# Merging five angles into the sine tables' instructions and reordering tile transposes in a gated state-space and feed-forward kernel

## The chip, the cores and the metric

The kernel runs on one core of one Trainium2 chip. The time is the device time of one execution in microseconds (us). A profile of one execution also has a span, from the first to the last instruction of the program; for this kernel it is about 1.8 us shorter than the time. TensorE is called PE in the profile, VectorE DVE, ScalarE ACT; PEld is PE's weight load.

## The reference

```python
x = A_x                                            # [1, 2048, 640], bf16
g = sigmoid((x * gate_w).sum(-1))                  # one gate per token
# a: state-space branch, 640 complex states
dt = exp(log_dt);  Lam_bar = exp(dt * (Lambda_re + 1j*Lambda_im))
h_t = Lam_bar * h_{t-1} + (B_bar @ x_t)            # over 2048 tokens
a = 2 * Re(C @ h) + x * Dskip
# b: feed-forward branch, 640 -> 1728 -> 640
b = gelu(x @ w1 + b1) @ w2 + b2
out = g * a + (1 - g) * b
```

## The kernel before

Tokens are handled in four chunks of 512, each of four tiles of 128. The recurrence is done by rotating with cosines and sines of `dt*Lambda_im*t`, so the kernel builds two tables, TCOS and TSIN, at its start. It takes sines for the first 64 angles of each state, then doubles the range three times with angle-addition formulas. These need the sine and cosine of five "span" angles (1, 512, 256, 128 and 64 steps).

Meanwhile PE must get going. The first chunk of x arrives with tokens on partitions and must be turned; PE does that with matmuls against an identity (`turn`), and DVE or ACT copies the result from PSUM to `xT[0]` (`turned`). Each of the four tiles has five 128-column blocks. `turn_first` does blocks 0 and 1, `turn_rest` blocks 2, 3 and 4. In the text, turn 2 is `turn_first(2)`, and the rest-turn of tile 2 is `turn_rest(2)`. Between turns PE does the feed-forward's first layer in strips: `part(kd, a)` is six matmuls of 128 columns into the six accumulators.

The kernel's PSUM pool has eight banks. Six are the accumulators, `pA` is a shared one, and so every `bank()` asked for by a turn gets the one that is left: a turn there must wait until the copy out of the turn before it has ended. I call it the rotating bank.

```python
def turn(p, col, a, kd):                                   # the matmul is L233 in the profile
    nc.tensor.matmul(p[:, col:col + P], lhsT=xn[0][:, a, kd*P:(kd+1)*P], rhs=ident[:], ...)

def turn_first(a, other):
    t = bank()
    turn(t, 0, a, 0)
    turned(nc.vector, t, 0, a, 0, 1)                       # DVE copy, L240
    turn(other, a * P, a, 1)
    turned(nc.scalar, other, a * P, a, 1, 2)               # ACT copy, L242
# ... cut ...
banks = [bank() for _ in range(FA)]                        # FA = 6 accumulators

def turn_rest(a, t, *parts):
    for k in range(KA, KD):                                # 2, 3, 4
        turn(t, (k - KA) * P, a, k)
    for engine, k0, k1 in parts:
        turned(engine, t, (k0 - KA) * P, a, k0, k1)
# ... cut; then the order in which PE gets its work (part's matmuls are L267):
part(0, 0); turn_first(1, pA); part(1, 0)
part(0, 1); turn_first(2, pA); part(1, 1)
turn_first(3, pA); part(0, 2)
turn_rest(0, bank(), (nc.scalar, KA, KD))
part(1, 2)
nc.tensor.matmul(pA[:, 0:3*KS], lhsT=prmA[:], rhs=ident[:, 0:3*KS], ...)   # the column matmul
nc.vector.tensor_copy(out=colA[:], in_=pA[:, 0:3*KS])
nc.scalar.activation(out=dt16[:], in_=ldt_c, func=ACT.Exp)                 # the dt exponential
# ... cut ...
part(0, 3)
turn_rest(1, bank(), (nc.vector, KA, KD))
part(1, 3)
turn_rest(2, pA, (nc.scalar, KA, KD))
part(2, 0)
turn_rest(3, bank(), (nc.vector, KA, KA + 1), (nc.scalar, KA + 1, KD))
# tables: u = angle in turns, kk = whole turns, red = rest, ab = |red|
nc.vector.tensor_tensor(out=u, in0=tf, in1=over(thp_c, HC), op=ALU.mult)    # 5 x 64 columns
nc.vector.tensor_copy(out=kk[:], in_=u)                                     # to int32
nc.vector.tensor_tensor(out=red, in0=u, in1=kk[:], op=ALU.subtract)
part(2, 1); part(2, 2); part(2, 3)
# ... two sine ACTIVATEs of 320 columns, then the same chain of 4 DVE and 2 ACT
#     instructions once more for the 5 x 5 span angles ...
```

## Time and profile before

| | before |
|---|---|
| time, median of 3 runs | 215.63 us (215.24 to 215.75) |
| span of the profiled run | 214.0 us |
| busy share | PE 98%, DVE 88%, ACT 48% |
| chain that ended last | PE 98% |
| 512-column matmuls, start to start | 215.6 ns |
| 128-column matmuls, start to start | 107 ns up to 5.5 us, 55.6 ns after |

The page of the kernel before has these lines on PE: busy time, share of the span and instructions, and further down the share of each engine in the chain of waits.

```profile
PE 210.5 (98%) x1407; PEld 126.5 (59%) x1407; DVE 189.4 (88%) x389; ACT 103.3 (48%) x188; POOL 1.0 (0%) x13
...
PE 98%; DVE 0%; issue 0%
```

PE is what bounds the kernel. "Busy" has to be read with care: a matmul's recorded duration (379 ns for 512 columns) is longer than the distance to the next (215.6 ns): the records of matmuls overlap, and the profile only models their ends. A short stall therefore hides inside the busy time. To find it one compares the start of a matmul with the start of the one before it. The timeline of the kernel before, from 5.7 to 9.4 us (columns: start in us, duration in us, engine, line, operation, names, shapes, count, and in brackets idle time before):

```profile
5.91 0.50 PE L267 MATMUL bank<-xT,w1a 128*128 128x128 bf16 x6
...
6.06 0.29 DVE L240 CAST xT<-bank 128x128 bf16<-128x128 f32 x1 [0.85 <-PE bank L233]
...
6.40 0.27 PE L233 MATMUL bank<-ident,xn 128*128 128x128 bf16 x2
...
6.51 0.50 PE L267 MATMUL bank<-xT,w1a 128*128 128x128 bf16 x6
6.66 0.29 DVE L240 CAST xT<-bank 128x128 bf16<-128x128 f32 x1 [0.31 <-PE bank L233]
...
7.00 0.33 PE L233 MATMUL bank<-ident,xn 128*128 128x128 bf16 x3
...
7.37 0.49 ACT L242 ACTIVATE xT<-bank 128x384 bf16<-128x384 f32 x1 [0.38 <-PE bank L233]
...
7.91 0.33 PE L233 MATMUL bank<-ident,xn 128*128 128x128 bf16 x3
...
8.94 0.33 PE L233 MATMUL bank<-ident,xn 128*128 128x128 bf16 x3
```

Six part matmuls start at 5.91, and 6 times 55.6 ns later, at 6.25, turn 3 could start; it starts at 6.40. That is just after DVE's copy of turn 2 (6.06 plus 0.29 is 6.35) has ended. The next turn likewise: 6.51 plus six matmuls is 6.85, and it starts at 7.00, after the copy that began at 6.66. From single matmuls, the stalls are 0.155 us at 6.40, 0.152 at 7.00, 0.046 at 7.91 and 0.032 at 8.94: 0.39 us, each at a turn. No bracket shows them, as PE counts as busy.

The table stage of the kernel before, in the same view:

```profile
10.03 0.33 DVE L387 CAST bu<-gel 128x320 int32<-128x320 f32 x1
...
11.33 0.47 ACT L392 ACTIVATE hs<-gel 128x320 f32<-128x320 f32 x1
11.33 0.18 DVE L395 TENSOR_TENSOR two<-thp_c,spans 128x25 f32<-128x25 f32 x1
...
12.16 0.21 ACT L400 ACTIVATE sq<-redq 128x25 f32<-128x25 f32 x1
...
12.59 1.28 ACT L272 ACT_TABLE_LOAD   x1
12.60 0.49 DVE L424 TENSOR_TENSOR gel<-hs,cq 128x320 f32<-128x320 f32 x1
```

L386 to L394 are the main chain, of 320 columns. L395 is the first of the span angles' own four instructions on DVE, L400 the first of their two on ACT, with 25 columns each; the four take 0.82 us from 11.33 to 12.15. L424 is the first doubling.

### The profile page before, as it was taken

Reading aid. Unit: us, or ns where it says so; the run is one execution under the profiler, and the core shown is the slowest. Engines: PE = TensorE matmul, PEld = TensorE weight load, DVE = VectorE, ACT = ScalarE, POOL = GpSimd, SP = SyncE. Lnnn points to the kernel's source line nnn. Section 1 sums busy time; section 2 is a strip of 40 time slices with the busy share of each in tenths; the row PEclk is TensorE's granted clock in tenths of the full one; section 3 lists DMA queues with packets and bytes.
Section 4 is the critical chain, followed back from the end, with each engine's and each line's share of the span. In section 5 each row is a group of like instructions: output and inputs, shape, how many; then the busy total and the mean of one; then the engine's idle time right before and its main releaser. Section 6 shows DMA issues by size and latency. Waiting matters only on the chain.

```text
span 214.0 us, 3599 instructions
## 1 busy us (share of the span) xinstructions
PE 210.5 (98%) x1407; PEld 126.5 (59%) x1407; DVE 189.4 (88%) x389; ACT 103.3 (48%) x188; POOL 1.0 (0%) x13
## 2 busy tenths in 40 slices
PE   8999999999999999999999999999999999999994
PEld 5945444454475644775457777444457687676773
DVE  2599999999998999999999999999999999993153
ACT  3599956675759579203573210455683422305100
POOL 1000000000000000000000000000000000000000
PEclk9999999999999999999999999999999999999999
DMA  6879999999000000052000006100000000110011
GB/s 192 222 178 190 201 156 246 347 207 230 1 0 0 3 0 0 14 152 96 0 0 3 0 0 180 68 0 2 3 0 14 0 3 31 61 34 0 0 66 61
DMA packets 31571, 15.84 MB, mean 74 GB/s; under 512 B 22978, under 2 KB 31554, under 8 KB 31554
## 3 DMA queue, kind: packets, MB, share of 16 engines
q1 hardware_dynamic: 30850, 14.99, 29.7%
q10 hardware_dynamic: 704, 0.62, 0.9%
q8 instruction: 11, 0.18, 0.4%
q14 instruction: 6, 0.05, 0.1%
HBM read 7.48 MB, written 2.62 MB: 47 GB/s over the span
## 4 chain that ended last, share of the span: by engine, by line
PE 98%; DVE 0%; issue 0%
PE bank L267 27%; PE bank L614 27%; PE bank L673 20%; PE bank L555 20%; PE bank L230 1%; PE bank L630 1%; PE bank L293 1%; PE bank L233 1%; DVE ot L678 0%; PE bank L362 0%; PE bank L283 0%; PE bank L404 0%; PE bank L373 0%
## 5 line engine op out<-in xcount | busy, mean ns | idle before, releaser
L614 PE MATMUL bank<-w_sb,gel 128*128 128x384 bf16 (+1 forms) x416 | 57.9, 300 | 0.0
L614 PEld LDWEIGHTS <-gel 128*128 128x128 bf16 x416 | 40.2, 98 | 17.1 <-issue 0.8
L558 ACT ACTIVATE bu<-bank 128x512 bf16<-128x512 f32 x40 | 23.7, 606 | 37.6 <-PE bank L555 37.6
L272 ACT ACTIVATE gel<-bank,colB 128x512 bf16<-128x512 f32 x52 | 33.6, 695 | 10.5 <-PE bank L267 10.2
L673 PEld LDWEIGHTS <-hs 128*128 128x128 bf16 x330 | 31.7, 98 | 11.7
L509 DVE TENSOR_TENSOR_SCAN g<-r_c,carry,v 128x512 bf16<-128x512 f32 x30 | 37.2, 1270 | 0.0
L622 ACT ACTIVATE gb<-bank,gcol 128x384 f32<-128x384 f32 (+1 forms) x32 | 15.1, 526 | 32.8 <-PE bank L614 16.6
L267 PE MATMUL bank<-xT,w1a 128*128 128x512 bf16 (+1 forms) x174 | 28.5, 319 | 0.0
L673 PE MATMUL bank<-CT_im,hs 128*128 128x320 bf16 (+2 forms) x165 | 27.1, 295 | 0.0
L673 PE MATMUL bank<-CT_re,hs 128*128 128x320 bf16 (+2 forms) x165 | 27.1, 295 | 0.0
L678 DVE SCALAR_TENSOR_TENSOR ot<-bank,gcol,gb 128x320 bf16<-128x320 f32 (+2 forms) x33 | 17.4, 533 | 9.8 <-PE bank L673 9.5
L555 PE MATMUL bank<-xT,BT_re 128*128 128x512 bf16 x100 | 24.9, 379 | 0.0
L555 PE MATMUL bank<-xT,BT_im 128*128 128x512 bf16 x100 | 24.9, 379 | 0.0
L267 PEld LDWEIGHTS <-w1a 128*128 128x128 bf16 x174 | 14.9, 101 | 11.6
L267 PE MATMUL bank<-xT,w1b 128*128 128x512 bf16 x80 | 17.9, 379 | 0.0
L555 PEld LDWEIGHTS <-BT_im 128*128 128x128 bf16 x100 | 9.8, 98 | 11.8
L588 DVE TENSOR_TENSOR bank<-xn,Dbc 128x320 f32<-128x320 bf16 (+2 forms) x33 | 14.5, 482 | 2.1 <-ACT gb L622 2.1
L555 PEld LDWEIGHTS <-BT_re 128*128 128x128 bf16 x100 | 9.6, 98 | 11.0
L490 DVE TENSOR_TENSOR v<-wa,wb 128x512 bf16<-128x512 bf16 x40 | 15.2, 421 | 0.6
L603 ACT ACTIVATE bank<-b2bc 128x384 f32<-128x384 bf16 (+1 forms) x24 | 11.7, 526 | 7.6 <-DVE ot L678 7.6
L490 DVE TENSOR_TENSOR wa<-TCOS,g 128x1024 bf16<-128x1024 bf16 x20 | 13.7, 686 | 0.1
L267 PE MATMUL bank<-xT,w1c 128*128 128x512 bf16 x60 | 13.7, 379 | 0.0
(103 smaller groups left out, 167.8 us busy)
## 6 DMA issues: line engine op xcount, KB each, us to landing
out_dram<-ot SPq DMA_DIRECT2D x15, 160.0 KB, 1.8
w_sb<-in_B_w_dram SPq DMA_DIRECT2D x1, 2080.0 KB
xn<-in_A_x_dram SPq DMA_DIRECT2D x3, 640.0 KB
w1b<-in_B_w_dram SPq DMA_DIRECT2D x5, 128.0 KB, 3.8
w1c<-in_B_w_dram SPq DMA_DIRECT2D x5, 112.0 KB, 4.3
w1a<-in_B_w_dram ACTq DMA_DIRECT2D x2, 192.0 KB, 3.0
w1a<-in_B_w_dram SPq DMA_DIRECT2D x1, 384.0 KB, 3.5
xn<-in_A_x_dram SPq DMA_DIRECT2D x4, 64.0 KB, 3.7
```

The costliest lines, as they stand in the source:

```text
L267: nc.tensor.matmul(p[:, t0:t1], lhsT=w, rhs=xT[c][:, kd, t0:t1], start=(kd == 0) if first is None else first, stop=(kd == last), skip_grou ...
L272: nc.scalar.activation(out=gel[c][:, kf, :], in_=p[:, :], func=ACT.Gelu_apprx_tanh, bias=b1_c[:, kf:kf + 1])
L490: nc.vector.tensor_tensor(out=o, in0=a, in1=b, op=op)
L509: nc.vector.tensor_tensor_scan(s["g"][:, ri, :], r_c[:, ks:ks + 1].to_broadcast([P, CH]), s["v"][:, ri, :], init, ALU.mult, ALU.add)
L555: nc.tensor.matmul(p[:], lhsT=BT[ks >= KSA][:, kd, (ks % KSA if ks < KSA else ks - KSA) * P:][:, 0:P], rhs=xT[c][:, kd, :], start=(kd == 0 ...
L558: nc.scalar.activation(out=bu[:, ri, :], in_=p[:], func=ACT.Identity)
L588: dve_now(ck.pe, 0.45, lambda: nc.vector.tensor_tensor(out=p[:, 0:d1 - d0], in0=xn[c][:, a, d0:d1], in1=Dbc[:, d0:d1], op=ALU.mult))
L603: nc.scalar.activation(out=v, in_=src, func=ACT.Identity)
L614: nc.tensor.matmul(p[:, col:col + d1 - d0], lhsT=gel[c][:, kf, a * P:(a + 1) * P], rhs=w2_sb[:, kf, d0:d1], start=False, stop=False, skip_ ...
L622: nc.scalar.activation(out=gbs[ti][:, d0:d1], in_=p[:, col:col + d1 - d0], func=ACT.Identity, scale=gcol[:, 1, ti:ti + 1])
L673: nc.tensor.matmul(p[:, 0:d1 - d0], lhsT=hs[c][:, j, lo:lo + P], rhs=CT[:, j % KS, d0:d1], start=False, stop=(j == 2 * KS - 1), skip_group ...
L678: nc.vector.scalar_tensor_tensor(out=ot[:, d0:d1], in0=p[:, 0:d1 - d0], scalar=gcol[:, 0, ti:ti + 1], in1=gbs[ti][:, d0:d1], op0=ALU.mult, ...
```

## The change

Two things. First, the five span angles become five more columns of the table: 5 x 69 columns instead of 5 x 64 and 5 x 5, so the chain of six small instructions goes. The doubling still wants them in another order, for which two small strided copies are added. Second, turn 2 moves ahead of `part(0, 1)`, and the rest-turn of tile 0 behind `part(1, 2)` and the column matmul, to where their banks are free. The aim is to have none of the stalls just shown.

```diff
-    spans = const.tile([P, NQ], F32, name="spans")
+    NP = NQ + HC
+    tf = const.tile([P, NP], F32, name="tf")         # 5 span factors, then 0..63
...
     turn_first(1, pA)
     part(1, 0)
+    turn_first(2, pA)
     part(0, 1)
-    turn_first(2, pA)
     part(1, 1)
     turn_first(3, pA)
     part(0, 2)
-    turn_rest(0, bank(), (nc.scalar, KA, KD))
     part(1, 2)
     nc.tensor.matmul(pA[:, 0:3 * KS], lhsT=prmA[:], ...)
     nc.vector.tensor_copy(out=colA[:], in_=pA[:, 0:3 * KS])
     nc.scalar.activation(out=dt16[:], in_=ldt_c, func=ACT.Exp)
     nc.vector.tensor_scalar(out=limp[:], in0=lim_c, scalar1=INV_2PI, ...)
+    turn_rest(0, bank(), (nc.scalar, KA, KD))
     part(0, 3)
...
-    nc.vector.tensor_tensor(out=u, ... to_broadcast([P, KS, HC]) ... over(thp_c[:], HC), op=ALU.mult)
+    nc.vector.tensor_tensor(out=u, ... to_broadcast([P, KS, NP]) ... over(thp_c[:], NP), op=ALU.mult)
...
-    nc.vector.tensor_tensor(out=two[:], ... thp_c x spans ..., op=ALU.mult)
-    nc.vector.tensor_copy(out=kq[:], in_=two[:])
-    nc.vector.tensor_tensor(out=redq[:], in0=two[:], in1=kq[:], op=ALU.subtract)
-    nc.vector.scalar_tensor_tensor(out=absq[:], ...)
-    nc.scalar.activation(out=sq[:], in_=redq[:], func=ACT.Sin, scale=TWO_PI_M)
-    nc.scalar.activation(out=cq[:], in_=absq[:], func=ACT.Sin, scale=-TWO_PI_M, bias=halfpi[:])
...
+    for dst, r in ((sq, 0), (cq, 1)):
+        nc.vector.tensor_copy(out=dst[:].rearrange("p (n k) -> p k n", n=NQ), in_=FSC[:, r*KS:(r+1)*KS, 0:NQ])
     double(HC, 4)
```

The rest-turn of tile 0 now stands in the program behind the dt exponential. Its copy is an ACT instruction, so on ACT, too, it comes after the exponential.

More of the change, by code (lines that the diff above doesn't have):

```diff
@@ L166 @@
     NQ = 5
-    spans = const.tile([P, NQ], F32, name="spans")
+    NP = NQ + HC
+    tf = const.tile([P, NP], F32, name="tf")
     for i, m in enumerate((1.0, float(CH), float(CH // 2), float(CH // 4), float(CH // 8))):
-        nc.gpsimd.memset(spans[:, i:i + 1], m)
+        nc.gpsimd.memset(tf[:, i:i + 1], m)
     nc.sync.dma_start(out=b1x[:, 0:F_LAST], in_=B_b1[F - F_LAST:F].rearrange("(o d) -> o d", o=1).to_broadcast([P, F_LAST]))
@@ L224 @@
     nc.vector.memset(halfpi[:], HALF_PI)
-    tf = const.tile([P, HC], F32, name="tf")
-    nc.vector.tensor_copy(out=tf[:], in_=tfi[:])
+    nc.vector.tensor_copy(out=tf[:, NQ:NP], in_=tfi[:])
     ones = lambda n: nc.const_aps.tensor(1.0, [P, n], BF16)
@@ L337, in scratch @@
     def scratch(i):
-        return scr[:, i * KS * P:i * KS * P + KS * HC].rearrange("p (k i) -> p k i", k=KS)
+        return scr[:, i * KS * P:i * KS * P + KS * NP].rearrange("p (k i) -> p k i", k=KS)
     u, red, ab = scratch(0), scratch(1), scratch(2)
-    FSC = hsp.tile([P, 2 * KS, HB], F32, name="hs")
-    FS = FSC[:, 0:KS, :]
-    FC = FSC[:, KS:2 * KS, :]
-    two = col("two", n=NQ * KS)
-    kq = col("kq", I32, n=NQ * KS)
-    redq = col("redq", n=NQ * KS)
-    absq = col("absq", n=NQ * KS)
+    FSC = hsp.tile([P, 2 * KS, NQ + HB], F32, name="hs")
+    FS = FSC[:, 0:KS, NQ:NQ + HB]
+    FC = FSC[:, KS:2 * KS, NQ:NQ + HB]
     sq = col("sq", n=NQ * KS)
     cq = col("cq", n=NQ * KS)
-    kk = work.tile([P, KS, HC], I32, name="bu", bufs=8)
+    kk = work.tile([P, KS, NP], I32, name="bu", bufs=8)
     sth, cth = sq[:, 0:KS], cq[:, 0:KS]
@@ L385 @@
     turn_rest(3, bank(), (nc.vector, KA, KA + 1), (nc.scalar, KA + 1, KD))
-    nc.vector.tensor_tensor(out=u, in0=tf[:].rearrange("p (o i) -> p o i", o=1).to_broadcast([P, KS, HC]), in1=over(thp_c[:], HC), op=ALU.mult)
+    nc.vector.tensor_tensor(out=u, in0=tf[:].rearrange("p (o i) -> p o i", o=1).to_broadcast([P, KS, NP]), in1=over(thp_c[:], NP), op=ALU.mult)
     nc.vector.tensor_copy(out=kk[:], in_=u)
@@ L391 @@
     part(2, 3)
-    nc.scalar.activation(out=FS[:, :, 0:HC], in_=red, func=ACT.Sin, scale=TWO_PI_M)
+    nc.scalar.activation(out=FSC[:, 0:KS, 0:NP], in_=red, func=ACT.Sin, scale=TWO_PI_M)
     nc.vector.scalar_tensor_tensor(out=ab, in0=red, scalar=-1.0, in1=red, op0=ALU.mult, op1=ALU.max)
-    nc.scalar.activation(out=FC[:, :, 0:HC], in_=ab, func=ACT.Sin, scale=-TWO_PI_M, bias=halfpi[:])
-    nc.vector.tensor_tensor(out=two[:].rearrange("p (n k) -> p n k", n=NQ), in0=thp_c[:].rearrange("p (o k) -> p o k", o=1).to_broadcast([P, NQ, KS]),
-                            in1=spans[:].rearrange("p (n o) -> p n o", o=1).to_broadcast([P, NQ, KS]), op=ALU.mult)
-    nc.vector.tensor_copy(out=kq[:], in_=two[:])
-    nc.vector.tensor_tensor(out=redq[:], in0=two[:], in1=kq[:], op=ALU.subtract)
-    nc.vector.scalar_tensor_tensor(out=absq[:], in0=redq[:], scalar=-1.0, in1=redq[:], op0=ALU.mult, op1=ALU.max)
-    nc.scalar.activation(out=sq[:], in_=redq[:], func=ACT.Sin, scale=TWO_PI_M)
-    nc.scalar.activation(out=cq[:], in_=absq[:], func=ACT.Sin, scale=-TWO_PI_M, bias=halfpi[:])
+    nc.scalar.activation(out=FSC[:, KS:2 * KS, 0:NP], in_=ab, func=ACT.Sin, scale=-TWO_PI_M, bias=halfpi[:])
     for kf in range(FA):
@@ L429, in double @@
         nc.vector.tensor_tensor(out=FS[:, :, hi], in0=m1, in1=m2, op=ALU.add)
+    for dst, r in ((sq, 0), (cq, 1)):
+        nc.vector.tensor_copy(out=dst[:].rearrange("p (n k) -> p k n", n=NQ), in_=FSC[:, r * KS:(r + 1) * KS, 0:NQ])
     double(HC, 4)
```

## The prediction

> **What bounds the kernel.** TensorE. The page has PE busy 98% of a 214.0 us span; the chain of waits is PE for 98%. Busy time alone proves little, so I took start-to-start gaps of matmuls from the timeline: from 9 us on a 512-column matmul starts every 215.6 ns, and no gap exceeds what its columns need, apart from the 64-row matmuls of L630. The Trainium skill ("TensorE: Matmul & The Clock Gate", back-to-back issue gap) gives N/2.4 + 2.5 ns, 215.7 for 512; the trace agrees. Nothing on DVE or ACT holds PE after 9 us, although DVE is 88% busy. Tightest: chunk 0's state matmuls (86.8 us) start 0.6 us after the last states are written.
>
> **Slack on PE before 9 us.** PE runs at half rate (107 ns per 128 columns) until 5.5 us, then 55.6. After that it stalls four times, each before a turn: 157 ns at 6.40, 154 at 7.00, 48 at 7.91, 34 at 8.94; 0.39 us together. Eight PSUM banks hold six accumulators, the shared bank, and one bank that all other turns share; each stall waits until DVE or ACT has copied that bank out.
>
> **Tables.** Removed: four small DVE operations (0.82 us from 11.33 to 12.15) and two ACT ones (0.42 us). Added: 25 columns on 320 in six operations (0.03 us each, from 0.48 us for 320) and two strided 25-element copies (0.18 us each). DVE is about even: the copies now stand between the w1c casts and the first doubling. The cast to int32 (0.33 us, below the 0.48 of two-operand work) should keep its rate: the skill ("VectorE: DVE Perf Modes", perf-mode tier table) allows odd extents when source and destination are equal. None of this is on PE's chain: worth 0.0 us.
>
> **Turns.** Turn 2 before part(0,1) is free at 5.43 (its load landed at 5.31). Turn 3 then has two parts between it and turn 2, so the 157 ns stall goes; the rest-turn of tile 0, after two parts and the column matmul, loses its 154 ns. But now only part(0,3), 0.33 us, lies between the rest-turns of tiles 0 and 1, which use the same bank. The copy between them takes ACT 0.49 us, and ACT's order now puts the dt exponential first, which waits for DVE's column copy (0.44 us from column matmul to exponential). Column matmul 7.02, exponential 7.47, copy 7.58 to 8.07, so rest-turn 1 starts about 8.1 instead of 7.91, after a stall of about 0.55 us. By then both kernels have done the same work. The 34 ns stall before rest-turn 3 disappears. Net: PE about 0.15 us later, carried to the end. The intended gain of 0.3 becomes a small loss.
>
> **Prediction.** 215.63 + 0.15: 215.8 us, range 215.2 to 216.4 (runs of before spread 0.5 us). Within 2%: 99%.
>
> **What would show it.** After: no gap before turn 3 and the rest-turn of tile 0; one gap of 0.4 to 0.65 us before the rest-turn of tile 1, released by ACT; rest-turn of tile 3 at 9.1 (8.94 before); sine ACTIVATEs of 345 columns 20 to 30 ns longer; gelu table load 0.1 to 0.2 us earlier than 12.59; no new PE gap after 9 us; chain still PE for 98%.
>
> **What would make it wrong.** The loads of tile 2 (landed 5.31) and of the columns (6.90) leave 0.1 us; later landings stall PE in the new order. ACT might reach tile 0's copy sooner, making a gain up to 0.3 us. The half-rate phase could end elsewhere, moving the span by more than the change.

## The result

| | median us | runs | lowest to highest |
|---|---|---|---|
| before | 215.72 | 6 | 215.24 to 216.06 |
| changed | 216.1 | 6 | 215.41 to 216.34 |

The ratio is 1.0012 with a 95% interval of 0.9991 to 1.0032: the same within 2%, and not told apart from zero by these runs. The spans of the two profiled runs are 214.02 and 214.21 us. The page of the changed kernel:

```profile
PE 209.7 (98%) x1396; PEld 126.6 (59%) x1407; DVE 188.9 (88%) x387; ACT 103.0 (48%) x186; POOL 1.0 (0%) x13
...
PE 98%; issue 0%; ACT 0%; DVE 0%
```

(Eleven of PE's 1407 matmul records are missing in this trace, which is the whole difference in the count; the loads are all there.) The timeline of the changed kernel, to be held against that of before; L368 is the column matmul:

```profile
6.27 0.28 PE L233 MATMUL bank<-ident,xn 128*128 128x128 bf16 x2
...
6.38 0.83 PE L267 MATMUL bank<-xT,w1a 128*128 128x128 bf16 x12
...
7.05 0.17 PE L368 MATMUL bank<-ident,prmA 128*128 128x15 bf16 x1
...
7.08 0.33 PE L233 MATMUL bank<-ident,xn 128*128 128x128 bf16 x3
...
7.24 0.50 PE L267 MATMUL bank<-xT,w1a 128*128 128x128 bf16 x6
...
7.61 0.47 ACT L242 ACTIVATE xT<-bank 128x384 bf16<-128x384 f32 x1
...
8.13 0.33 PE L233 MATMUL bank<-ident,xn 128*128 128x128 bf16 x3 [0.39 <-ACT xT L242]
...
9.13 0.33 PE L233 MATMUL bank<-ident,xn 128*128 128x128 bf16 x3
```

Turn 3 at 6.27 and the rest-turn of tile 0 at 7.08 follow their predecessors without a gap. The rest-turn of tile 1 could start at 7.24 + 6 x 55.6 ns = 7.58 and starts at 8.13: a stall of 0.553 us, with idle time that the bracket lays to ACT. The chain of waits of the changed kernel, from 7.2 us on (start, us, what), says how it is made; L369 is the column copy on DVE, L370 the dt exponential:

```profile
7.21 0.05 PE bank L368
...
7.29 0.19 DVE colA L369
...
7.49 0.21 ACT dt L370
7.70 0.39 ACT xT L242
...
8.13 0.33 PE bank L233 x3
```

PE's chain now leaves PE for 0.84 us: column matmul, copy on DVE, exponential on ACT, copy of tile 0 on ACT, and only then the next rest-turn. The rest-turn of tile 3 is at 9.13 (8.94 before), and the 0.19 us stay to the end: the last matmul starts at 211.25 us in the changed kernel and at 211.06 before. From 9 us on there is no stall in either trace apart from the same small ones at the half-row matmuls (64 rows).

The table stage of the changed kernel:

```profile
10.25 0.34 DVE L383 CAST bu<-gel 128x345 int32<-128x345 f32 x1
...
11.52 0.49 ACT L388 ACTIVATE hs<-gel 128x345 f32<-128x345 f32 x1
...
12.51 1.28 ACT L272 ACT_TABLE_LOAD   x1
12.52 0.19 DVE L421 COPY cq<-hs 128x25 f32<-128x25 f32 x1
...
12.74 0.49 DVE L413 TENSOR_TENSOR gel<-hs,cq 128x320 f32<-128x320 f32 x1
```

The chain of six is gone, the sine instructions have 345 columns, and two copies (L421; the second is shown) precede the first doubling (L413). The doubling starts at 12.74 instead of 12.60, but PE, too, runs 0.19 us later here. Gelu's table load starts 0.08 us earlier by the clock, about 0.28 us earlier relative to PE. Nothing comes of that: PE wasn't waiting for it.

### The profile page after: what moved, and what is told of

It reads as the page before. It is cut to its first block, busy times and chain, and to the rows that moved or that the text cites. A ratio compares the mean times of both kernels' runs of the same rounds, so it can differ in the third digit from the quotient of the medians.

```text
span 214.2 us, 3585 instructions
## 1 busy us (share of the span) xinstructions
PE 209.7 (98%) x1396; PEld 126.6 (59%) x1407; DVE 188.9 (88%) x387; ACT 103.0 (48%) x186; POOL 1.0 (0%) x13
## 4 chain that ended last, share of the span: by engine, by line
PE 98%; issue 0%; ACT 0%; DVE 0%
PE bank L605 27%; PE bank L267 26%; PE bank L664 20%; PE bank L546 20%; PE bank L230 1%; PE bank L621 1%; PE bank L293 1%; PE bank L233 1%; ACT xT L242 0%; DVE ot L669 0%; PE bank L358 0%; ACT dt L370 0%; DVE colA L369 0%; PE bank L283 0%; PE bank L368 0%
```

## The experiments

The theory: the change acts through the rotating bank. It takes away 0.31 us of stalls in front of turn 3 and of the rest-turn of tile 0, and makes a new one of 0.55 us in front of the rest-turn of tile 1, as only one part (0.33 us) is left to hide a copy that takes 0.47 us and stands behind the exponential. The tables are off PE's chain. The rivals: the tables make the difference; the difference is scatter; PE waits for something other than ACT.

### The change in halves

The first run has the tables of the change and the turn order of before; the second the reverse.

```diff
 # tables only, against the changed kernel
-    turn_first(2, pA)
     part(0, 1)
+    turn_first(2, pA)
     part(1, 1)
     turn_first(3, pA)
     part(0, 2)
+    turn_rest(0, bank(), (nc.scalar, KA, KD))
     part(1, 2)
     # column matmul, its copy, dt exponential, limp
-    turn_rest(0, bank(), (nc.scalar, KA, KD))
```

The turns-only kernel is the reverse: these lines as in the changed kernel, all table lines as in the kernel before.

> The table half of the change alone, with the turns of the kernel before. Theory (the change acts on TensorE through the turns' PSUM bank, and the tables are off its chain): the same stalls before the turns as before (about 0.15, 0.15, 0.05 and 0.03 us), first w1b matmul at 12.7 us as before (within 0.05), span 214.0 us, ratio 1.000. Rival A (the tables matter: fewer DVE and ACT operations make it faster, or the later doubling makes it slower): a span at least 0.15 us away from before although PE's stalls before 9.2 us are the same.

Measured: 215.68 us median of 6, against 215.78 of 11 runs of before; ratio 0.9996 (0.9979 to 1.0014). The stalls in the trace are 0.154, 0.157, 0.047 and 0.035 us, as before; the first w1b matmul starts at 12.68, the span is 213.96. (w1b holds the weights of the next four column blocks of the first layer; its first matmul comes after all turns and parts and so marks when PE is through this stage.) So the tables neither help nor hurt.

> The turn half of the change alone, with the tables of the kernel before. Theory: no stall before turn 3 and before the rest-turn of tile 0, one stall of about 0.55 us before the rest-turn of tile 1, released by ACT's copy of tile 0; first w1b matmul 0.15 to 0.2 us later than before (12.9), span about 214.2 us, ratio about 1.001. Rival A (tables made the 0.2 us): first w1b matmul at 12.7 us, span 214.0. Rival B (the whole 0.2 us is scatter of loads and clock phase from run to run): any value between 213.6 and 214.6, without relation to the stalls.

Measured: 215.80 us median of 6; ratio 1.0007 (0.9987 to 1.0027). The stall in front of the rest-turn of tile 1 is 0.552 us, those in front of turn 3 and the rest-turn of tile 0 are gone, the span is 214.12. The first w1b matmul is at 12.83, not quite the 12.9 expected; why is told under "Accounting" below. The stall belongs to the turn order. What the times can't do is to show the 0.2 us, and of rival B (scatter) a part is true: the six spans of this program went from 213.8 to 214.8.

### The exponential behind the copy

```diff
-    nc.scalar.activation(out=dt16[:], in_=ldt_c, func=ACT.Exp)
     nc.vector.tensor_scalar(out=limp[:], ...)
     turn_rest(0, bank(), (nc.scalar, KA, KD))
+    nc.scalar.activation(out=dt16[:], in_=ldt_c, func=ACT.Exp)
```

> The changed kernel with one line moved: the dt exponential stands behind the copy of tile 0's rest-turn on ACT instead of ahead of it, the bank is still shared. Theory (the stall is the bank's occupancy, and the exponential ahead of the copy is a third of it): the copy starts about 7.43 us, the rest-turn of tile 1 about 7.98 us after a stall of about 0.4 us, first w1b matmul about 12.77 us, span about 0.15 us shorter than the changed kernel, ratio to before about 1.000. Rival C (PE waits for something else, such as the load of the second half of the rest columns): the rest-turn of tile 1 stays at 8.1 us.

Measured: 216.05 us median of 6; ratio 1.0008 (0.9990 to 1.0027). In the timeline of this kernel the copy now stands first:

```profile
7.70 0.49 ACT L242 ACTIVATE xT<-bank 128x384 bf16<-128x384 f32 x1 [0.58 <-PE bank L233]
...
8.09 0.20 ACT L372 ACTIVATE dt<-colA 128x5 bf16<-128x5 f32 x1
8.24 0.33 PE L233 MATMUL bank<-ident,xn 128*128 128x128 bf16 x3 [0.24 <-ACT xT L242]
```

The stall is 0.406 us, as expected, and ends with the copy, so rival C falls: PE's start moves with ACT's order. But the absolute times expected (7.98 for the turn, 12.77 for w1b) were missed by 0.26 us: 8.24 and 13.03. In this run PE went to full rate only at 6.04 us, not 5.52. And the time is no shorter than that of the changed kernel, since 0.15 us are below what six runs can tell.

### Three bank assignments

The rest-turn of tile 1 needn't use the rotating bank: the shared bank is free as soon as the columns are copied out. This exchanges the two banks.

```diff
-    turn_rest(1, bank(), (nc.vector, KA, KD))
+    turn_rest(1, pA, (nc.vector, KA, KD))
     part(1, 3)
-    turn_rest(2, pA, (nc.scalar, KA, KD))
+    turn_rest(2, bank(), (nc.scalar, KA, KD))
     part(2, 0)
-    turn_rest(3, bank(), (nc.vector, KA, KA + 1), (nc.scalar, KA + 1, KD))
+    turn_rest(3, pA, (nc.vector, KA, KA + 1), (nc.scalar, KA + 1, KD))
```

> The changed kernel with three bank assignments changed: the rest-turn of tile 1 goes into the shared bank (free once the column copy has ended, about 7.46 us), that of tile 2 into the rotating bank (free about 8.1 us), that of tile 3 into the shared bank. Theory: no stall above 0.05 us before any turn from 5.5 us on, last turn about 8.7 us (9.25 in the changed kernel, 9.05 before), first w1b matmul about 12.35 us, span 0.55 us shorter than the changed kernel and 0.35 shorter than before, about 213.65 us, ratio to before about 0.998. Rival D (PE is freed but another wait takes the time back, such as the loads of w1a rows 3 and 4 landing at 8.8 us or the first gelu releasing its bank): the last turn is at 8.7 us, but a new gap opens before 16 us and the span is within 0.1 us of before.

Measured: the last turn is at 8.68, w1b at 12.35, the span is 213.64, all as expected. The time isn't: 215.87 us median of 6 against 215.78, ratio 1.0001 (0.9982 to 1.0021). And one expectation failed in the trace: a stall of 0.216 us at 5.41. It is at turn 2. The timeline has DVE's copy of turn 1 and the weight load of turn 2, which reads x:

```profile
5.01 0.29 DVE L240 CAST xT<-bank 128x128 bf16<-128x128 f32 x1 [0.88 <-PE bank L233]
...
5.41 0.11 PEld L233 LDWEIGHTS <-xn 128*128 128x128 bf16 x2 [0.23 <-DMA xn<-in_A_x_dram]
```

The wait that ended last is that for its load of x, which this order needs earlier than the one before. But the rotating bank would have held turn 2 nearly as long. DVE's copy of turn 1 ended at 5.30, and where the data were in time (see "Once more, for the times") turn 2 starts 0.05 us after that copy: here it would be at 5.35, so that the bank alone makes about 0.15 of the 0.22 us. PE had gone to full rate early in this run, at 4.71 us, and then the one part between turns 1 and 2 is too short to cover the copy. So the span was right because things happened to cancel: compared with the changed kernel, early full rate saved 0.50 us, turn 2's new stall cost 0.22, and the first turn came 0.17 late. No new gap opened after 9 us, so rival D (a later wait takes the gain back) has no support in the trace.

### Accounting

These traces differ in the moment of full rate, 4.71 to 6.51 us over ten of them. Up to then a 128-column matmul takes 107 instead of 55.6 ns. The Trainium skill ("TensorE: Matmul & The Clock Gate", "What's actually happening") says that the clock is released after a busy window of 3413 ns that runs freely, so that the moment varies from run to run. That it varies the traces show; no run here shows the window itself. The profile's PEclk (the granted clock) doesn't show this phase: it reads 1.00 for 4.40 to 5.50 us of the kernel before, where matmuls start 107 ns apart. The rate has to be taken from the starts. One can add up, from the starts of the matmuls: when the first turn starts, what the half rate cost up to its end, and the stalls up to the first 512-column matmul of the real work. What is left of the span should be the same for every kernel.

| kernel | full rate from | first turn | half-rate loss | stalls | span | span less the three |
|---|---|---|---|---|---|---|
| before | 5.50 | 3.29 | 0.96 | 0.55 | 214.02 | 209.23 |
| before, again | 5.95 | 3.33 | 1.14 | 0.55 | 214.26 | 209.24 |
| tables only | 5.39 | 3.31 | 0.88 | 0.56 | 213.96 | 209.21 |
| changed | 5.52 | 3.33 | 0.94 | 0.72 | 214.21 | 209.23 |
| changed, again | 6.51 | 3.28 | 1.43 | 0.71 | 214.66 | 209.24 |
| turns only | 5.17 | 3.41 | 0.73 | 0.75 | 214.12 | 209.23 |
| exponential behind | 6.04 | 3.34 | 1.18 | 0.57 | 214.31 | 209.22 |
| banks exchanged | 4.71 | 3.50 | 0.44 | 0.46 | 213.64 | 209.24 |
| banks exchanged, again | 6.02 | 3.30 | 1.19 | 0.21 | 213.92 | 209.22 |
| exchanged, old tables | 4.84 | 3.35 | 0.59 | 0.35 | 213.54 | 209.25 |

All in us; "stalls" counts what exceeds 25 ns, and includes 0.16 us in front of the first part matmul in every row, so the stalls before of 0.39 and the changed kernel's 0.55 stand here as 0.55 and 0.72. The last column lies within 0.04 us. So in these ten traces everything that tells one kernel or run from another happens before the first 512-column matmul and is one of three things; old or new tables make no difference. The change itself is worth 0.72 - 0.55, so +0.17 us, and the exchanged banks 0.21 - 0.55, so -0.34 us, less the wait in front of turn 2 (0.14 and 0.22 us) in runs with early full rate. That wait comes from moving turn 2 ahead, so the changed kernel must expect it too: with an early full rate it would lose about 0.17 + 0.14, or 0.31 us. This is an estimate from these traces, and takes it that the kernel before keeps its 0.55; neither trace of the changed kernel had full rate before 5.5 us. The half-rate loss alone differs by 1.0 us, more than any of these.

### An attempt to take the scatter away

If real work always ran at full rate, times would show the difference. I put eight throwaway matmuls ahead of the first turn that read weights as they land, the last at about 8.9 us, into four kernels. One of them has a throwaway ACT instruction as well, to make the suspected wait longer.

```diff
+    for w, n in ((w1a[1], 2), (w1a[2], 3), (x rest columns, 2), (w1a34, 1)):
+        for _ in range(n):
+            nc.tensor.matmul(pA[:, 0:512], lhsT=w[128 x 128], rhs=ones(512), start=True, stop=True)
     turn_first(0, pA)
 # and in the fourth:
     nc.scalar.activation(out=dt16[:], in_=ldt_c, func=ACT.Exp)
+    nc.scalar.activation(out=junk[:], in_=ones(512), func=ACT.Identity)
```

> The kernel before with eight more 512-column throwaway matmuls ahead of the first turn; they read weights and x as these land, so the last one waits for the load that lands at about 8.9 us and the real work starts at about 9.1 us, always at full rate. Theory for the scatter (the moment at which TensorE goes to full rate, 4.75 to 6.08 us in the six profiles so far, differs from run to run and is most of the scatter of about 1 us): the six spans of this kernel lie within 0.35 us of each other; span about 218.6 us. Rival (scatter comes from loads or from later stages): the spans still spread by 0.7 us or more.

> The changed kernel with the same eight throwaway matmuls. Theory: the stall before the rest-turn of tile 1 is 0.55 us, and counted from the first turn every later matmul is 0.15 to 0.19 us later than in the warm version of the kernel before; the mean times of the two warm versions differ by 0.1 to 0.25 us with little scatter. Rival (the 0.2 us was scatter): the means differ by less than 0.05 us.

> The version with the three bank assignments changed, with the same eight throwaway matmuls. Theory: counted from the first turn, the last turn and all later matmuls are 0.3 to 0.4 us earlier than in the warm version of the kernel before and 0.5 to 0.55 us earlier than in the warm version of the changed one, and the mean times differ by the same. Rival (PE's gain is given back, as the timed runs without the extra warm-up seemed to show: 215.87 against 215.78 us): the last turn is earlier, but the mean time is within 0.1 us of the warm version of the kernel before.

> The changed kernel with the eight throwaway matmuls and one throwaway 512-column ACT operation between the dt exponential and the copy of tile 0's rest-turn, so that the bank is held longer. Theory: the copy starts about 0.5 us later, the stall before the rest-turn of tile 1 grows from 0.55 to about 1.07 us and the mean time by the same 0.5 us against the warm version of the changed kernel. Rival (ACT does not set that start, or PE has slack later): the stall or the span grows by less than 0.25 us.

Measured, medians: 221.30 us (4 runs) for before, 222.64 (6) for the changed kernel, 221.46 (6) for the exchanged banks, 223.42 (5) for the longer wait; ratios to the plain kernel before 1.0263, 1.0323, 1.0277 and 1.0360. As a way to take scatter away this failed: the runs of one kernel still spread by 0.8 us (before) to 2.1 us (exchanged banks), and the spans are 218.77 to 222.10 us instead of about 218.6. The first of these kernels shows what happened, in the table of time windows (PEclk is the granted clock):

```profile
core 0: us, PE busy (x) PEld busy (x) DVE busy (x) ACT busy (x) POOL busy (x), PEclk, DMA share, GB/s
4.00:7.30 3.30, 1.61 (x6) 0.44 (x7) 0.00 (x0) 0.00 (x0) 0.00 (x0) 1.00 0.84 258
7.40:10.70 3.30, 2.90 (x21) 1.97 (x20) 0.58 (x2) 0.48 (x2) 0.00 (x0) 0.50 0.90 256
10.80:14.00 3.20, 3.20 (x54) 2.97 (x53) 1.37 (x7) 1.46 (x5) 0.00 (x0) 1.00 0.86 188
```

In the first window PE worked for only half of the time, waiting for loads between the throwaway matmuls, and in the next window it had half the clock. The starts agree with PEclk here: two throwaway matmuls in a row are 220 to 227 ns apart in the first window, and from 7.4 us on 128-column matmuls are 107 ns apart. The real work ran at half rate until about 10.8, 13.96, 9.7 and 14.1 us in the four traces, and their spans (219.39, 221.30, 218.77 and 222.10 us) have the same order. So the warm-up brought on the thing that it was to prevent, and the mean times of these four say nothing about 0.2 us.

Their traces still answer two questions, as the stall in front of the rest-turn of tile 1 fell after full rate in all of them. The changed kernel with warm-up (L371 is the column matmul here, L242 the copy):

```profile
14.19 0.33 PE L233 MATMUL bank<-ident,xn 128*128 128x128 bf16 x3
...
14.71 0.47 ACT L242 ACTIVATE xT<-bank 128x384 bf16<-128x384 f32 x1
...
15.24 0.33 PE L233 MATMUL bank<-ident,xn 128*128 128x128 bf16 x3 [0.39 <-ACT xT L242]
```

and the one with the throwaway ACT operation (L375):

```profile
14.45 0.33 PE L233 MATMUL bank<-ident,xn 128*128 128x128 bf16 x3
...
14.98 0.61 ACT L375 ACTIVATE junk<-const-bfloat16-1.0 128x512 bf16<-128x512 bf16 x1
...
15.50 0.47 ACT L242 ACTIVATE xT<-bank 128x384 bf16<-128x384 f32 x1
...
16.02 0.33 PE L233 MATMUL bank<-ident,xn 128*128 128x128 bf16 x3 [0.91 <-ACT xT L242]
```

The copy starts 1.05 us after the rest-turn of tile 0 instead of 0.52, and the stall is 1.07 us instead of 0.55: it grew by as much as the copy was put off. That PE waits there for this copy on ACT is shown. The times of the two (222.64 and 223.42) are in the right order, but too scattered to confirm the size. In the third kernel no rest-turn waits longer than 0.05 us; its turn 2 waits 0.154 us for the rotating bank, since at full rate one part doesn't cover the copy of turn 1.

### Once more, for the times

> The changed turn order with the three exchanged bank assignments, but the tables of the kernel before. Theory: no stall of 0.1 us or more from a bank before any turn; set against the kernel before, and corrected for the moment at which TensorE goes to full rate (half of that moment's difference), the last turn is 0.35 us earlier. The mean time is 0.15 to 0.4 us below that of the kernel before, less than in the trace because in runs that go to full rate late the kernel before has fewer stalls. Rival A (the tables of the change carry part of the swap's gain): the last turn is as early, but a gap opens between 12 and 17 us, or the span is 0.15 us or more longer than that of the swapped version with new tables, corrected likewise.

The edit is the exchange of banks in the turns-only kernel. Measured: 215.38 us median of 6 against 215.63 of 11; ratio 0.9995 (0.9975 to 1.0014). No gap opens from 12 to 17 us, so rival A falls again. But no stall of 0.1 us or more from a bank was expected, and there is one of 0.136 us, in front of turn 2:

```profile
4.97 0.29 DVE L240 CAST xT<-bank 128x128 bf16<-128x128 f32 x1 [1.00 <-PE bank L233]
...
5.12 0.29 PEld L233 LDWEIGHTS <-xn 128*128 128x128 bf16 x2
5.31 0.27 PE L233 MATMUL bank<-ident,xn 128*128 128x128 bf16 x2
```

The data were there, as turn 2's first weight load starts at 5.12. Turn 2 itself starts at 5.31, after the copy of turn 1 has ended at 5.26. So it is the rotating bank once more: full rate came at 4.84 us, and at full rate one part doesn't cover that copy, as in the third kernel with warm-up. The last matmul of the last turn is at 8.57 us against 9.05. Corrected for the moment of full rate (0.66 us earlier, so 0.33) that is 0.15 us earlier, not the 0.35 expected: the first turn was 0.07 us later, and turn 2 waited those 0.14 us. The mean, 215.50 us, is 0.12 below that of the 11 runs of before beside it, short of the 0.15 expected.

> The swapped version once more, the same program as before, to settle whether its time is below that of the kernel before, since the first six runs (mean 215.74 us against 215.79) could not tell 0.3 us from nothing. Theory: over these and the first runs together the mean is 0.15 to 0.4 us below that of the kernel before. Rival D (the gain is given back): the means agree within 0.1 us.

Measured: 215.67 us median of 5; ratio 0.9998 (0.9984 to 1.0012). The timeline of this run, for the turns that had stalled:

```profile
7.30 0.33 PE L233 MATMUL bank<-ident,xn 128*128 128x128 bf16 x3
...
7.80 0.33 PE L233 MATMUL bank<-ident,xn 128*128 128x128 bf16 x3
...
8.36 0.33 PE L233 MATMUL bank<-ident,xn 128*128 128x128 bf16 x3
...
8.86 0.33 PE L233 MATMUL bank<-ident,xn 128*128 128x128 bf16 x3
```

From 7.30 to 7.80 there are three matmuls of the turn and six of a part, 9 x 55.6 ns, and no stall; the rest-turn of tile 2 at 8.36 has 0.049 us. The three rest-turns come 0.50, 0.56 and 0.50 us after each other; in the changed kernel the first of these distances was 1.05. In the times the expectation failed: over its 11 runs this program has a mean of 215.68 us, against 215.71 for the 22 runs of before beside them. That is what rival D expected of the means, though no trace shows a later wait that takes the gain back.

> The changed kernel once more, the same program, beside the two others on one chip. Theory: a stall of 0.55 us before the rest-turn of tile 1 whatever the moment of full rate, and over all its runs a mean 0.1 to 0.3 us above that of the kernel before. Rival (no difference): the means agree within 0.05 us over all runs.

Measured: 216.25 us median of 6; ratio 1.0021 (1.0003 to 1.0039), now clear of zero. Full rate came at 6.51 us in the trace, a whole microsecond later than in its first one, and the stall is 0.549 us all the same.

All runs of a program together: the changed kernel has a mean of 216.03 us over 12, the kernel before 215.71 over 39, so the change costs 0.32 us with an estimated standard error of 0.13, against 0.17 by stalls in the traces (0.1 to 0.3 was expected). With exchanged banks, old and new tables, it is 215.62 over 17: 0.41 us below the changed kernel with an estimated standard error of 0.14, but only 0.09 below the kernel before, with 0.09. Whether it beats the kernel before is open. The traces say 0.34 us when full rate comes after turn 2, and 0.12 to 0.20 when it comes before 5 us and turn 2 has to wait; the times say less.

> The kernel before once more, for a second trace with another moment of full rate. Theory: the bank of turn 2 is released a fixed 0.6 us after its matmul, so the stall before turn 3 depends on the rate at which the part between them runs: 0.15 us if full rate comes before about 5.8 us, and less, down to nothing, if it comes after 6.2 us; the stalls of 0.05 us or less further on stay as they were. The span moves by half of the change of that moment, less what the stall gives back: about 213.7 us for 4.8, 214.1 for 6.0, 214.3 for 6.6. Rival (the stalls are fixed amounts): 0.15 us before turn 3 at any moment of full rate.

Measured: one run, 216.04 us, beside 216.39 for the same program. Full rate came at 5.95 us and the stall in front of turn 3 is 0.154 us. The span is 214.26, 0.24 above that of the first trace, which is half of the 0.45 us by which full rate was later, with nothing given back by the stall. This tells nothing apart: the part in front of turn 3 ran after 6.0 us, at full rate, so both readings expect 0.15. That late full rate hides the stalls of the kernel before, which would explain why its mean is so near that of the exchanged banks, is only argued. Turn 2's wait in runs with early full rate is a part of the explanation that two of the three traces with exchanged banks do show.

## Why the prediction was right

- **Time and class.** 215.8 us, 215.2 to 216.4, 99% within 2%: the median is 216.1, and the ratio 1.0012. This says little by itself: the median of every kernel here without warm-up (215.38 to 216.25 us) lies in the range. What was put to the test is the stall.
- **PE bounds the kernel, DVE and ACT don't.** Right. Tables alone: the same time, and the same remainder in the accounting. The skill's N/2.4 + 2.5 ns, which its section calls the isolated case, held: 215.7 against 215.6 ns in the trace.
- **The stalls before, and the two that go.** Right: no gap in front of turn 3 at 6.27 and of the rest-turn of tile 0 at 7.08.
- **The new stall.** Right in place, cause and size: 0.55 us and a start at about 8.1 were predicted, 0.553 us and 8.13 measured. That the start, too, was right is luck: full rate came at 5.52 us in this trace and at 5.50 before. In the second trace it came at 6.51, and the rest-turn started at 8.59, after the same stall. What made it possible was to follow a bank to its *next* user, and to read in ACT's order that the exponential precedes the copy. The copy began at 7.61 (predicted 7.58), 0.11 us after an exponential of 0.21 us: ACT instructions overlap by about 0.1 us, which agrees with the 93 ns of the skill ("ScalarE: Activation LUTs", "What ACT_TABLE_LOAD costs").
- **The net of 0.15 us, carried to the end.** The traces have 0.19, of which 0.17 are stalls and the rest start and clock. The times have 0.38 between the medians and 0.32 over all runs, with an error of 0.13.
- **Table costs.** The sines grew by 25 and 23 ns (20 to 30 predicted). The cast to int32 of 345 columns takes 343 ns against 327 for 320, so 25 columns more cost it 16 ns, against 27 in the first two-operand multiply (481 to 508). It kept its rate with an odd extent, as read from the skill ("VectorE: DVE Perf Modes", "What auto-detection actually checks"). The two copies took 0.18 and 0.19 us.
- **A small miss.** Gelu's table load was to start 0.1 to 0.2 us earlier and started 0.08 earlier. In the trace, doing without the small sines frees ACT 0.32 us sooner, the longer sines take 0.05 back, and the sine table load is 0.19 late (10.03 before, 10.23 after), as PE's new stall delays the last turn's copy on ACT. The prediction doesn't say of what its 0.1 to 0.2 was made, so which of these it had wrong stays open.
- **What was not seen.** Turn 2 "is free at 5.43" reckons with its load and the half rate only. With full rate at 4.84 us, turn 2 waited 0.136 us for the rotating bank in the kernel with exchanged banks and old tables, whose turns up to there are the changed kernel's. The stall taken away in front of turn 3 had come back in front of turn 2. That it did not do so in the traces of the changed kernel is again a matter of when full rate came.
- **What was feared.** That the end of the half-rate phase moves the span by more than the change is what happens, in both directions and for each kernel; a range of 0.6 us either side was needed.

## What to carry to other kernels

When a matmul is moved to where its buffer is free, ask who uses that buffer next: a stall that is removed in one place can come back, larger, at the next user, and the copy in between runs in its engine's program order, so one instruction issued ahead of it is part of the wait. Whether a gap in the order covers a copy depends on the rate at which the work in it runs: check it at full rate too. On the engine that bounds the kernel, look for stalls in start-to-start distances, as its busy time hides those that are shorter than the overlap of the records: none of the four stalls before shows in a bracket, and of the 0.55 us only 0.39 do. When the effect is below the scatter of the times, take the scatter apart in the traces first; here three sums left the same remainder of ten spans to within 0.04 us, where a dozen timed runs hardly told the sign.

## What the Trainium skill lacked or had wrong

- "TensorE: Matmul & The Clock Gate", "Back-to-back issue gap": for a stream of weight load and matmul pairs it gives sustained distances of about 131 ns (N=512) and 81 ns (N=128) and calls N/2.4 + 2.5 ns the isolated case. Here pairs run at 215.6 and 55.6 ns over the whole kernel, so the "isolated" formula is the one that holds.
- The same page, "What's actually happening": it has the moment of full rate vary by 500 ns either way and the ramp cost below 1%. Ten traces had the moment between 4.71 and 6.51 us, a wider range of 1.8 us, and the loss between 0.44 and 1.43 us of 214. The loss is below 1%, but it is most of the scatter between traces, and the page doesn't say that it can hide a change of this size.
- The same page: it doesn't say how busy a window must be. PE was busy for 1.61 of 3.30 us in one window, with no two matmuls more than 1.25 us apart, and got half the clock in the next; in two kernels PE was then busy for about 2.9 of 3.3 us (7.4 to 10.7 us), and one was back at full rate at 10.8 us, the other at 13.96.
- No page that I read gives the time in which a PSUM bank comes back to PE. From the first matmul into it to the next one: 0.60 us with a DVE copy of 128 columns, 0.91 with an ACT copy of 384, 1.05 with an exponential ahead of that copy, 1.04 with a DVE copy of 384.
